# Attention and mixture of experts on one core: moving the first turns of each head pair behind its own joint tile, and the third and fourth tiles' turns into one run

## The chip, the cores and the metric

The kernel runs on one core of a Trainium2 chip. A core has TensorE (PE in the profile, its weight loads PEld), VectorE (DVE), ScalarE (ACT), GpSimd (POOL) and SyncE (SP), which here issues transfers. Each engine has its own queue and works through it in order; semaphores tie the queues together. The metric is the device time of one execution in microseconds (us), lower being better.

## The reference

Causal attention with a decay over 8 batches, 8 heads, 576 positions and 64 channels a head, then a mixture of eight experts, of which each token takes one:

```python
scores = scale * np.matmul(q, k.transpose(0, 1, 3, 2))
log_f = np.log(np.clip(f, 0.0001, 1.0))
cum = np.cumsum(log_f, axis=-1)
decay = cum[:, :, :, None] - cum[:, :, None, :]
scores = np.where(causal, -1000000000.0, scores + decay)
attn = softmax(scores)                    # over the last axis
attn_out = np.matmul(attn, v)
...
x = attn_out.transpose(0, 2, 1, 3).reshape(B * S, H * D)
logits = x @ w_gate
expert_idx = np.argmax(logits, axis=1)    # gate_w: its softmax probability
...
h = np.maximum(xe @ w1[e], 0.0)
out[mask] = gate_w[mask, None] * (h @ w2[e])
```

## The kernel before

Attention runs over 32 pairs of heads, four to a batch, in `attention_all`; the experts follow (`Moe`), from about 320 us on. The attention loop has a step for each pair n and each i from 0 to 6 (two more rounds of it drain the pipeline). The order that the code issues in is pinned on every engine (`InOrder`), so each engine's queue is what the loop writes.

A pair's scores come as tiles of 128 queries, named head and row block: 03 and 13 are 512 keys wide, 02 and 12 are 384 wide (with 00 and 10, 128 wide, in the same PSUM bank), 01 and 11 are 256 wide and share a bank. The last 64 queries of both heads make one joint tile (J), in two halves of 288. For each tile TensorE does the score matmuls (`smm`, L414, two passes of operands named qk and k,q), VectorE adds the mask and takes the row minimum while it copies the scores to SBUF (`s_red`, L421, a reduction and a short read of its accumulator), and ScalarE takes the exponential in place (`s_exp`, L428). `s_steps(n)` lists these for i = 0 to 5: 03; 13; 02 with 00; 12 with 10; 01 with 11; J.

The probabilities are then turned, that is transposed on TensorE against the identity (`turn`, L477), into a PSUM bank and copied from there to the tile aT (L471 on VectorE, L473 on ScalarE). `t_steps(n - 1)` lists the turns of the pair before, one item for each i of pair n: first 03, second 13, third 02 with 00, fourth 12 with 10, then `t_one` for 01 with 11, then the joint tile. ScalarE copies the 512- and 384-wide ones, VectorE the two 128-wide ones (00, 10) and t_one's. The turns share the pool `ps_t` of two PSUM banks: a turn's bank is that of the turn two before it. Score tiles share three banks (`ps_s`).

At i = 1 of pair n, `av(n - 2)` multiplies the turned probabilities by v (L553), into the banks `ps_v` and `ps_m`, one each, and ScalarE copies them out (L561).

Once a batch's four pairs are through, `fin_tasks(b)` spreads its routing over the next four pairs and a little beyond, in a list of (pairs later, i, task), with g the number of the first of them:

- `fin_x(b, t)` turns a block of x rows (`xT`) and VectorE scales it into a row tile (L599), which goes to DRAM three steps later (`c.later`, L607). Its bank is `ps_v` or `ps_m`.
- `fin_gate` (L623) and `fin_logits` make the router's logits: turns of gT, then VectorE's products (L641).
- `softmax`, `expert`, `gate`, `rank`, `slot`, `hi`, `lo` and `table` rank the tokens for the experts. `rank` has matmuls L935 and L937 and VectorE's L942 to L950; `hi` a one-hot on VectorE (L972) and five products on GpSimd (L979); `lo` a one-hot on VectorE (L986); `table` the matmuls L993.

Also in a pair, GpSimd splits the next pairs' operands into high and low parts (L330, L369, L379), and VectorE does one cast of k (L373, `k_first`).

Of the kernel before, what the change touches and what calls it, by code (L numbers as in the profile page):

```python
# [174 lines left out]
def attention_all(c, tc, qkT, va, vb, f, wgd, x_dram, batch_done, more_consts, extra):  # L175
# [15 lines left out]
    with ExitStack() as st:  # L191
# [15 lines left out]
        def step(f):  # L207

            if pe_last:
                with tc.issue_after(pe_last[0]):  # L210
                    f()
            else:
                f()
# [370 lines left out]
        def fin_x(b, t, scalar=False, bank=None):  # L584
            xT, rinv = xTws[b], rinvs[b]
            qs, qn = QS[t], QN[t]

            px = psum(ps_s if (b, t) == (B - 2, 0) or b == B - 1 and t > 1
                      else bank or fin_bank[0])
            for p in range(NPAIR):  # L590
                turn(px[:qn, P * p : P * p + P], xT[:, p, qs : qs + qn])
            xr = row_tile(c)
            if scalar:
                for h in range(H):
                    hs = slice(h * HD, h * HD + HD)
                    nc.scalar.activation(xr[:qn, hs], px[:qn, hs], AF.Copy,
                                         scale=rinv[:qn, t, h : h + 1])
            else:
                V.tensor_tensor(  # L599
                    xr[:qn].rearrange("q (h d) -> q h d", d=HD),  # L600
                    px[:qn].rearrange("q (h d) -> q h d", d=HD),
                    rinv[:qn, t, :].unsqueeze(2).to_broadcast([qn, H, HD]), ALU.mult,
                )
            r0 = b * S + qs

            def write():
                nc.sync.dma_start(x_dram[r0 : r0 + qn, :], xr[:qn])  # L607


            if b < B - 2:  # L610
                c.later.append([3, write])
            else:
                write()
# [16 lines left out]
        def fin_logits(b, part, bank=None):  # L630
            rinv = rinvs[b]
            if part == 0:
                lgs[b] = (c.ps_r[:, 0:40].rearrange("p (t e) -> p t e", e=8),
                          sm.tile([P, 5, 8, 8], F32, name="gq", bufs=1))
            lg, gq = lgs[b]
            pg = psum(bank or fin_bank[0])
            tiles = (0, 1, 2, 3) if part == 0 else (4,)
            for i, t in enumerate(tiles):
                turn(pg[:, P * i : P * i + P], gTw[part][:, P * i : P * i + P])
            for i, t in enumerate(tiles):  # L640
                V.tensor_tensor(  # L641
                    gq[:, t],
                    pg[:, P * i : P * i + P].rearrange("q (h e) -> q e h", e=16)[:, 0:8, :],
                    rinv[:, t, :].unsqueeze(1).to_broadcast([P, 8, 8]), ALU.mult,
                )
            if part == 1:
                V.tensor_reduce(lg, gq, AX.X, ALU.add)
# [4 lines left out]
        def fin_tasks(b):  # L652

            (softmax, expert, gate, rank, slot, hi, lo, table), after = batch_done(
                b, lambda: lgs[b][0]
            )
            fx = [lambda t=t: fin_x(b, t, b == B - 1 and t > 0) for t in range(5)]
            lg = [lambda p=p: fin_logits(b, p) for p in range(2)]  # L660
            g = NPAIR * b + 6
            if b == B - 1:
                return dict(fx=fx, lg=lg, softmax=softmax, expert=expert, gate=gate,
                            rank=rank, slot=slot, hi=hi, lo=lo, table=table,
                            logits=lambda: fin_gate(b))
            r = [(0, 3, lg[0]), (1, 0, lambda: fin_logits(b, 1, ps_m)), (1, 1, softmax),
                 (1, 1, expert), (2, 1, gate)]

            if b < B - 2:
                among[g + 1, 3] = [rank]  # L670
                late = int(b < B - 1 - LATE)
                r += [(0, 2, fx[0]), (0, 4, fx[1]), (2, 2, fx[2]), (2, 3, fx[3]), (3, 1, slot),
                      (3 + late, 1, lo), (3, 2, hi), (4, late, table)]
                r += [(4, 0, lambda: fin_x(b, 4, bank=ps_m)) if late else (3, 3, fx[4])]
            else:
                r += [(2, 0, rank), (2, 1, slot), (2, 2, fx[0]), (2, 3, hi), (2, 3, lo),
                      (2, 3, fx[1]), (2, 4, fx[2]), (2, 5, fx[3]), (2, 6, fx[4]),
                      (3, 0, table)]
            for dn, i, f in r + after:

                at, i = (among, ~i) if i < 0 else (tasks, i)
                at.setdefault((g + dn, i), []).append(f)
# [40 lines left out]
        def c_writes():  # L723
# [4 lines left out]
            sp_dma(ck[:, :, 1, 0:512], cwf[NPR:NH, :, 0:512])  # L728
            sp_dma(ck[:, :, 1, 512:], cwf[NPR:NH, :, S:640])
        tasks, among, c.later, order = {}, {}, [], InOrder(tc)  # L730
        c.note = note
        for n in range(NP + 2):
            b, p = divmod(n, NPAIR)
            if n < NP and p == 0:
                xTs[b], xTws[b] = (
                    t["xT", (b + 1) % 2].rearrange("p (n s) -> p n s", s=S)
                    for t in (c.values, c.words)
                )
                ssums[b] = sm.tile([P, 5, H], F32, name="ssum")
                V.memset(ssums[b][64:128, 4, :], 1.0)  # L740
                jsums[b] = sm.tile([P, NPAIR], F32, name="jsum")
            ss = s_steps(n) if n < NP else []
            ts_ = t_steps(n - 1) if 0 < n <= NP else []
            for i in range(7):
                for x in c.later:
                    x[0] -= 1
                while c.later and c.later[0][0] <= 0:
                    c.later.pop(0)[1]()
                if n == 0:
                    if i == 0:  # L750
                        first_q(1)
                        late_consts()
                    elif i == 2:
                        second_q(1)
                    elif i == 3:
                        first_k(1)
                    elif i == 5:
                        second_k(1)
                elif n + 1 < NP:
                    if i == 0 and n > 1:  # L760
                        load_c(n + 1)
                    elif i == 0:
                        c_rows(2, 0)
                        c_rows(2, 1)
                        load_pair(3)
                        c_writes()
                    elif i == 2:
                        copies(n + 1)
                if i in (2, 4) and 2 <= n < 5:
                    next(c.more, None)  # L770
                if i == 5 and n + 2 < NP:
                    q_parts(n + 2)
                if i == 5 and n == 2:
                    load_gate()
                if i == 3 and n < NP:
                    load_v(n)
                if i == 2 and 0 < n < NP - 3:
                    load_pair(n + 3)
                s_, e_ = ss[i] if ss else (None, None)
                if s_:  # L780
                    step(s_)
                for f in among.pop((n, i), []):
                    step(f)
                if ts_ and ts_[i]:
                    step(ts_[i])

                if e_:
                    e_()
                if i == 1 and 0 < n and n + 1 < NP:
                    k_first(n + 1)  # L790
                if i == 1 and 2 <= n:
                    step(lambda: av(n - 2))
                    av_out()


                    fb, fp = divmod(n - 2, NPAIR)
                    if fp == 0 and 1 <= fb:
                        step(lambda: fin_gate(fb - 1))
                        fin_tasks(fb - 1)
                    elif fp == NPAIR - 1 and fb == B - 1:  # L800
                        todo = fin_tasks(fb)

                fin_bank[0] = (ps_v, ps_m)[i % 2]
                for f in tasks.pop((n, i), []):
                    step(f)
                at = {(0, 1): 0, (1, 0): 1, (1, 1 if b == B else 5): 2}.get((p, i))
                if n >= NPAIR and at is not None:
                    fin_sums(b - 1, at)
                if (n, i) == (NP, 0):
                    scores.close()  # L810
                for f in extra(n, i):
                    step(f)
                order.pin()
                if (n, i) == (NP + 1, 1):
                    break
# [961 lines left out]
```

## Time and profile before

| what | value |
|---|---|
| median of three runs | 791.38 us (791.35 to 792.48) |
| the profiled execution, its own time | 791.58 us |
| its span in the profile | 789.8 us |
| granted TensorE clock | 0.999 |
| PE, DVE, ACT, POOL busy | 768.5, 587.0, 511.2, 543.8 us |
| turns (L477), PE, first two head-0 tiles: 03 and 02 | 15.6 and 16.3 us in 128 turns each |

A row of the timeline has start and duration in us, engine, line, operation, what it writes and reads, shapes, count, and in brackets the idle time before it with what ended it. The 128x512 and the like after the operation are partitions and elements. Matmuls are pipelined and their ends are modelled, so TensorE is read by its starts. A group of waits has the waiting engine and line, what it waited for, the sum in us, the count, and the longest.

### The profile page before, as it was taken

Reading aid. Unit: us, or ns where it says so; the run is one execution under the profiler, and the core shown is the slowest. Engines: PE = TensorE matmul, PEld = TensorE weight load, DVE = VectorE, ACT = ScalarE, POOL = GpSimd, SP = SyncE. Lnnn points to the kernel's source line nnn. Section 1 sums busy time; section 2 is a strip of 40 time slices with the busy share of each in tenths; the row PEclk is TensorE's granted clock in tenths of the full one; section 3 lists DMA queues with packets and bytes.
Section 4 is the critical chain, followed back from the end, with each engine's and each line's share of the span. In section 5 each row is a group of like instructions: output and inputs, shape, how many; then the busy total and the mean of one; then the engine's idle time right before and its main releaser. Section 6 shows DMA issues by size and latency. Waiting matters only on the chain.

```text
span 789.8 us, 16191 instructions
## 1 busy us (share of the span) xinstructions
PE 768.5 (97%) x5496; PEld 672.3 (85%) x5496; DVE 587.0 (74%) x1654; ACT 511.2 (65%) x1278; POOL 543.8 (69%) x466
## 2 busy tenths in 40 slices
PE   4999999999999999999999999999999999999996
PEld 3888888888888888888999899898898998998985
DVE  6688989898989899755589848578497487485630
ACT  6798888888888888944466546366366465463621
POOL 6999898989898989753487647556565575475311
PEclk9999999999999999999999999999999999999999
DMA  7998877787787874533445362353433433523200
GB/s 182 224 208 188 198 182 189 188 185 183 180 200 174 203 173 120 178 114 118 124 134 160 107 198 83 103 189 93 143 105 107 156 93 107 181 70 110 98 28 32
DMA packets 66825, 114.70 MB, mean 145 GB/s; under 512 B 8295, under 2 KB 39015, under 8 KB 63412
## 3 DMA queue, kind: packets, MB, share of 16 engines
q1 hardware_dynamic: 59700, 93.71, 45.8%
q0 software_dynamic: 6400, 19.93, 7.8%
q8 instruction: 44, 0.72, 0.4%
q14 instruction: 41, 0.34, 0.1%
q10 hardware_dynamic: 640, 0.01, 0.0%
HBM read 94.05 MB, written 20.55 MB: 145 GB/s over the span
## 4 chain that ended last, share of the span: by engine, by line
PE 89%; DVE 6%; ACT 2%; POOL 1%; SPq 1%; issue 1%; DMA 1%; POOLq 0%; DVEq 0%; ACTq 0%
PE ps L1200 29%; PE ps L1400 19%; PE ps L414 14%; PE ps L553 10%; PE ps L477 9%; PE ps L1170 4%; PE pr L1400 1%; DVE sc L421 1%; PE ps L1356 1%; DVE qk L373 1%; ACT sc L428 1%; DVE aT L471 1%; SPq L217 1%; ACT aT L473 1%; PE pr L993 1%
## 5 line engine op out<-in xcount | busy, mean ns | idle before, releaser
L428 ACT ACTIVATE sc<-sc,nmx 128x512 f32<-128x512 f32 (+3 forms) x256 | 142.3, 558 | 7.3 <-DVE nmx L421 5.5
L414 PE MATMUL ps<-qk 128*128 128x288 f32 (+4 forms) x384 | 124.9, 356 | 10.7 <-ACT qk L355 10.4
L421 DVE CUSTOM_DVE_ANT_0 sc<-ps,mask 128x512 f32<-128x512 f32 (+3 forms) x256 | 115.1, 483 | 16.4 <-PE ps L414 15.1
L1200 PE MATMUL ps<-w_0w,hhw 128*128 128x512 f32 x280 | 112.9, 403 | 0.0
L1400 PE MATMUL ps<-X_0w,w1s 128*128 128x320 f32 x504 | 111.7, 309 | 0.0
L1200 PE MATMUL ps<-w_0w,hl 128*128 128x512 f32 x280 | 110.8, 396 | 0.0
L1200 PE MATMUL ps<-w_1w,hhw 128*128 128x512 f32 x280 | 110.4, 394 | 0.0
L414 PE MATMUL ps<-k,q 68*128 68x288 f32 (+4 forms) x384 | 107.2, 327 | 1.5 <-DMA q<-xT0w 1.5
L1208 POOL DMA_INDIRECT out<-y,si_fast x37 | 37.3, 1009 | 96.6 <-ACT y L1207 87.6
L473 ACT COPY aT<-ps 128x512 f32<-128x512 f32 (+1 forms) x156 | 82.8, 531 | 20.4 <-PE ps L477 20.2
L553 PE MATMUL ps<-aT,va_t 128*64 128x256 f32 (+3 forms) x896 | 94.6, 354 | 0.0
L330 POOL TENSOR_TENSOR k<-raw,qk 64x1152 fp32r<-64x1152 f32 x30 | 79.8, 2659 | 18.4 <-DVE qk L373 18.4
L330 POOL TENSOR_TENSOR qk<-raw,qk 64x1280 fp32r<-64x1280 f32 x30 | 88.1, 2936 | 2.4
L1400 PEld LDWEIGHTS ps<-X_0w,w1s 128*128 128x128 f32 x504 | 84.3, 188 | 0.0
L414 PEld LDWEIGHTS ps<-qk 128*128 128x128 f32 x384 | 71.1, 197 | 14.1 <-ACT qk L355 10.4
L1207 ACT ACTIVATE y<-ps,g_fast 128x512 f32<-128x512 f32 x37 | 25.5, 690 | 87.0 <-PE ps L1200 64.9
L553 PEld LDWEIGHTS ps<-aT,va_t 128*64 128x64 f32 x896 | 58.9, 137 | 26.0 <-issue 0.7
L1400 PE MATMUL ps<-X_1w,w1s 128*128 128x320 f32 x252 | 77.9, 309 | 0.0
L414 PEld LDWEIGHTS ps<-k,q 68*128 68x128 f32 x384 | 72.7, 199 | 3.0 <-issue 2.6
L1447 POOL TENSOR_TENSOR u<-u,u 128x320 f32<-128x320 f32 x27 | 23.7, 878 | 60.6 <-DVE u L1445 60.3
L1200 PEld LDWEIGHTS ps<-w_0w,hl 128*128 128x128 f32 x280 | 52.5, 187 | 12.8
L1200 PEld LDWEIGHTS ps<-w_1w,hhw 128*128 128x128 f32 x280 | 52.8, 189 | 11.0
(242 smaller groups left out, 1900.6 us busy)
## 6 DMA issues: line engine op xcount, KB each, us to landing
raw<-in_qkT SPq DMA_DIRECT2D x52, 608.0 KB
w1r<-in_w SPq DMA_DIRECT2D x112, 128.0 KB
w<-in_w SPq DMA_DIRECT2D x28, 512.0 KB
va_t<-in_va SPq DMA_DIRECT2D x32, 256.0 KB
x_dram<-row SPq DMA_DIRECT2D x32, 256.0 KB
raw<-in_qkT SPq DMA_DIRECT2D x12, 320.0 KB
wraw<-in_w SPq DMA_DIRECT2D x7, 512.0 KB
raw<-in_qkT SPq DMA_DIRECT2D x12, 288.0 KB
```

Of the source, the lines that this page charges most:

```text
L330: return eng.tensor_tensor(o, raws[n][p0 : p0 + 64, c0:c1], ops[n][0][p0 : p0 + 64, c0:c1].bitcast(F32), ALU.subtract,)
L414: note(nc.tensor.matmul(out, ql[:, q0 : q0 + P], kl[:, j, k0 : k0 + kw], start=(i == 0), stop=(i == last),))
L421: V.tensor_tensor_reduce(dst[:, 0 : src.shape[1]], src, m, -0.125, init, ALU.add, ALU.min, nms[n][:, col : col + 1],)
L428: nc.scalar.activation(x, x, AF.Exp, bias=nms[n][:, col : col + 1], scale=-1.0, accum_out=acc)
L473: nc.scalar.copy(dst, src)
L477: note(nc.tensor.transpose(out.bitcast(F32R), words, c.identr))
L553: c.last_av = note(nc.tensor.matmul(pv[j * HD : (j + 1) * HD, q0 - qa : qb - qa], l, r, start=(blk == 0), stop=(blk == nb - 1),))
L1170: c.note(nc.tensor.matmul(ph[:, 0:n], w[:, wi, fs], x[xi][:, kt, :], start=(k == 0), stop=(k == 3 * KT - 1),))
L1200: c.note(nc.tensor.matmul(py, rows(hi_, ft), w[wi], start=(ft + k == 0), stop=(ft == FT - 1 and k == 2),))
L1207: nc.scalar.activation(y, py, AF.Copy, scale=g[:, s : s + 1])
L1208: nc.gpsimd.indirect_dma_start(out=self.out, out_offset=bass.IndirectOffsetOnAxis(ap=si[:, s : s + 1], axis=0), in_=y, in_offset=None, bou ...
L1400: self.nc.tensor.matmul(bank[:, 0:HN], w[:, wi, mat, kt], x[xi][:, kt, :], start=start and k == 0, stop=k == 5, skip_group_check=True,)
```

## The change

The first turns of a pair (03) move from the next pair's i = 0 to the pair's own i = 5, right behind the joint tile's turns of its predecessor. The third turns (02, 00) move from i = 2 to i = 3, so that they and the fourth run together. The exponentials of the third tile (02, 00) are held until after the fourth turns' copies. Of the routing, the logits' second part moves from the start of the next pair to i = 5, the first and third rows of x move a step later, behind the fourth turns, the fifth row moves from the next pair's i = 0 to i = 5, and each row has its bank fixed. The last batches keep their banks.

```diff
+            fx = [(lambda t=t, k=k: fin_x(b, t, bank=k))
+                  for t, k in enumerate((ps_v, ps_v, ps_v, ps_m, ps_m))] if b < B - 2 else fx
-            r = [(0, 3, lg[0]), (1, 0, lambda: fin_logits(b, 1, ps_m)), (1, 1, softmax),
+            r = [(0, 3, lg[0]), (0, 5, lambda: fin_logits(b, 1, ps_m)), (1, 1, softmax),
                  (1, 1, expert), (2, 1, gate)]
...
-                r += [(0, 2, fx[0]), (0, 4, fx[1]), (2, 2, fx[2]), (2, 3, fx[3]), (3, 1, slot),
+                r += [(0, 3, fx[0]), (0, 4, fx[1]), (2, 3, fx[2]), (2, 3, fx[3]), (3, 1, slot),
                       (3 + late, 1, lo), (3, 2, hi), (4, late, table)]
-                r += [(4, 0, lambda: fin_x(b, 4, bank=ps_m)) if late else (3, 3, fx[4])]
+                r += [(3, 5 if late else 3, fx[4])]
...
+        turns = {1: (1,), 3: (2, 3), 4: (4,), 5: (5,)}
+        held = []
...
+            if ts_:
+                ts_[0] = None
...
-                if ts_ and ts_[i]:
-                    step(ts_[i])
-
-                if e_:
+                for k in (turns if n < NP else {i: (i,)}).get(i, ()) if ts_ else ():
+                    if ts_[k]:
+                        step(ts_[k])
+                if i == 5 and n < NP:
+                    step(t_steps(n)[0])
+
+                if e_ and i == 2 and ts_:
+                    held.append(e_)
+                elif e_:
+                    while held:
+                        held.pop()()
                     e_()
```

On TensorE, in a pair without rows of x at this place, from the third score tile (02 with 00) to t_one's scores; sc_02w and sc_12w are the third and fourth turns:

```order
 L414 MATMUL ps<-qk_1300 128x128
 L414 MATMUL ps<-k_1_208,q_1_206 128x128
-L477 MATMUL ps<-identr,sc_02w 128x128 x4
 L414 MATMUL ps<-qk_1300 128x384
 L414 MATMUL ps<-k_1_208,q_1_206 128x384
 L414 MATMUL ps<-qk_1300 128x128
 L414 MATMUL ps<-k_1_208,q_1_206 128x128
+L477 MATMUL ps<-identr,sc_02w 128x128 x4
 L477 MATMUL ps<-identr,sc_12w 128x128 x4
 L414 MATMUL ps<-qk_1300 128x256
```

The third turns now stand behind the fourth tile's scores, in one run with the fourth turns.

On VectorE at the same place of such a pair; the ISA rows are the reductions of a tile and their reads, the copies of 128x128 are those of 00 and 10:

```order
 L421 ISA sc_02_73,nmx<-ps,mask 128x128
 L421 ISA nmx 128x1
-L471 COPY aT_91<-ps 128x128
 L421 ISA sc_12_79,nmx<-ps,mask 128x384
 L421 ISA nmx 128x1
 L421 ISA sc_12_79,nmx<-ps,mask 128x128
 L421 ISA nmx 128x1
-L471 COPY aT_91<-ps 128x128
+L471 COPY aT_91<-ps 128x128 x2
 L421 ISA sc_01_75,nmx<-ps,mask 128x256
 L421 ISA nmx 128x1
```

The copy of 00 now stands behind the fourth tile's two reductions.

On TensorE, from the joint turns of the pair before (sc_Jw) into the next pair's first scores:

```order
 L477 MATMUL ps<-identr,sc_Jw 68x128
 L477 MATMUL ps<-identr,sc_Jw 128x128 x4
+L477 MATMUL ps<-identr,sc_03w 128x128 x4
 L414 MATMUL ps<-qk_325 128x512
 L414 MATMUL ps<-k_0_207,q_0_205 128x512
-L477 MATMUL ps<-identr,sc_03w 128x128 x4
 L414 MATMUL ps<-qk_325 128x512
 L414 MATMUL ps<-k_0_207,q_0_205 128x512
```

The first turns (sc_03w) moved from between the two 512-wide score tiles to right behind the joint turns, ahead of both.

## The prediction

> **What bounds the kernel now.** I read the engines' shares on the page first, then the chain that ended last, then TensorE's own waits, and last, for four attention pairs in a row, the stretch from a pair's third score tile to the next pair's attention times values.
>
> ```profile
> PE 768.5 (97%) x5496; PEld 672.3 (85%) x5496; DVE 587.0 (74%) x1654; ACT 511.2 (65%) x1278; POOL 543.8 (69%) x466
> PE 89%; DVE 6%; ACT 2%; POOL 1%; SPq 1%; issue 1%; DMA 1%; POOLq 0%; DVEq 0%; ACTq 0%
> ...
> PE pr L993 <- DVE Ar L986: 2.1, 5, 0.4
> ...
> PEld ps L477 <- DVE aT L471: 3.2, 16, 0.2
> ```
>
> TensorE is busy 97% of the span and holds 89% of the chain. Inside attention its only listed waits are the five at the routing table (L993), 0.42 us each. The last row is the warning: 16 times a turn's weight load already sat still until VectorE had copied an older turn out of PSUM (L471).
>
> The four stretches, with columns of width, then busy time of PE, PEld, DVE, ACT and POOL, then the granted clock (1.00 throughout):
>
> ```profile
> 182.85:189.10 6.25, 6.25 (x58) 5.88 (x54) 5.26 (x24) 5.50 (x19) 5.84 (x7) 1.00 0.71 157
> 194.02:201.31 7.29, 7.29 (x65) 6.82 (x62) 6.60 (x28) 4.84 (x16) 7.15 (x4) 1.00 0.37 124
> 204.18:210.57 6.39, 6.39 (x59) 5.90 (x55) 5.80 (x32) 5.50 (x21) 6.31 (x3) 1.00 0.89 182
> 213.44:220.15 6.71, 6.71 (x61) 6.31 (x57) 6.36 (x28) 5.51 (x20) 6.48 (x6) 1.00 0.87 208
> ```
>
> I call them by what rides along: the plain pair, the logits pair (two rows of x and the logits), the rank pair, the rows pair (two rows of x). They repeat with each batch. TensorE never stops in them, and VectorE rests only 0.99, 0.69, 0.59 and 0.35 us. So TensorE sets the pace, and VectorE, which empties PSUM, is close behind: an order that makes TensorE need a bank earlier, or VectorE free it later, costs at once.
>
> **The change part by part.** First the saving. TensorE's rows of the plain pair:
>
> ```profile
> 182.85 0.44 PE L414 MATMUL ps<-qk 128*128 128x384 f32 x1
> ...
> 183.82 0.41 PE L414 MATMUL ps<-qk 128*128 128x384 f32 x1
> 184.07 0.34 PE L414 MATMUL ps<-k,q 68*128 68x384 f32 x1
> 184.25 0.22 PE L414 MATMUL ps<-qk 128*128 128x128 f32 x1
> ...
> 185.31 0.29 PE L477 MATMUL ps<-identr,sc_01w 128*128 128x128 f32 x2
> ...
> 186.74 0.54 PE L477 MATMUL ps<-identr,sc_Jw 128*68 128x128 f32 x5
> 187.12 0.46 PE L414 MATMUL ps<-qk 128*128 128x512 f32 x1
> ...
> 188.19 0.45 PE L414 MATMUL ps<-qk 128*128 128x512 f32 x1
> 188.48 0.39 PE L414 MATMUL ps<-k,q 68*128 68x512 f32 x1
> 188.71 0.46 PE L477 MATMUL ps<-identr,sc_13w 128*128 128x128 f32 x4
> ```
>
> Starts are compared, since ends are modelled. A score matmul right behind a turn takes 0.25 us (183.82 to 184.07), its equal behind another score matmul 0.18 (184.07 to 184.25); at 512 columns 0.29 against 0.23. The new order takes two such switches out of each pair: the fourth tile's scores now follow the third's, and the second 512-wide tile follows the first. That is 0.07 + 0.06 = 0.13 us a pair. For 31 pairs that alone is 4.0 us.
>
> [...]
>
> Now the price. The turns share two PSUM banks in rotation, so a turn needs the bank of the turn two before it, and its copies out. VectorE's rows of the plain pair:
>
> ```profile
> 183.69 0.56 DVE L421 CUSTOM_DVE_ANT_0 sc<-ps,mask 128x384 f32<-128x384 f32 x1 [0.65 <-PE ps L414]
> 184.17 0.08 DVE L421 DVE_READ_ACCUMULATOR2_ANT nmx<- 128x1 f32 x1
> ...
> 184.38 0.08 DVE L421 DVE_READ_ACCUMULATOR2_ANT nmx<- 128x1 f32 x1
> 184.53 0.29 DVE L471 COPY aT<-ps 128x128 f32<-128x128 f32 x1
> 184.74 0.36 DVE L972 TENSOR_TENSOR eqh<-pr,iotah 128x200 bf16<-128x200 f32 x1
> 185.01 0.55 DVE L421 CUSTOM_DVE_ANT_0 sc<-ps,mask 128x384 f32<-128x384 f32 x1
> ...
> 186.10 0.41 DVE L421 CUSTOM_DVE_ANT_0 sc<-ps,mask 128x256 f32<-128x256 f32 x1
> ...
> 186.78 0.69 DVE L471 COPY aT<-ps 128x512 f32<-128x512 f32 x1
> ```
>
> A tile's two reductions take 0.48 + 0.21 = 0.69, a small copy 0.21 to the next start (0.29 to its end), the one-hot (L972) 0.27, the two 256-wide reductions 0.68, the 512-wide copy 0.69. VectorE starts 0.84 after the third tile's first matmul, because it waits for the scores, and will again.
>
> *Plain pair.* The small copy of the third turns, which frees the bank of t_one's turns (sc_01w), now stands behind the one-hot and the fourth tile's reductions: it ends at 0.84 + 0.69 + 0.27 + 0.69 + 0.29 = 2.78. TensorE wants the bank at 185.31 - 182.85 - 0.07 = 2.39. Wait 0.39; behind it queue t_one, the joint scores and all that follows on TensorE. Net 0.39 - 0.13 = +0.26. Before, the copy ended at 184.82, half a microsecond ahead of need.
>
> The logits pair needs rows of its own, three of VectorE's and three of TensorE's:
>
> ```profile
> 194.83 0.56 DVE L421 CUSTOM_DVE_ANT_0 sc<-ps,mask 128x384 f32<-128x384 f32 x1
> ...
> 197.44 0.61 DVE L641 TENSOR_TENSOR gq<-ps,rinv 128x64 f32<-128x64 f32 x4
> 197.96 0.41 DVE L421 CUSTOM_DVE_ANT_0 sc<-ps,mask 128x256 f32<-128x256 f32 x1
> ...
> 197.46 0.50 PE L477 MATMUL ps<-identr,xT0w 128*128 128x128 f32 x4
> ...
> 200.14 0.25 PE L477 MATMUL ps<-identr,gT1w 128*128 128x128 f32 x1
> 200.36 0.50 PE L414 MATMUL ps<-qk 128*128 128x512 f32 x1
> ```
>
> and so do the rank pair (206.83 to 208.73) and the rows pair (from 216.81), TensorE's and VectorE's:
>
> ```profile
> 206.83 0.29 PE L477 MATMUL ps<-identr,sc_01w 128*128 128x128 f32 x2
> ...
> 208.26 0.54 PE L477 MATMUL ps<-identr,sc_Jw 128*68 128x128 f32 x5
> 208.73 0.47 PE L414 MATMUL ps<-qk 128*128 128x512 f32 x1
> ...
> 206.90 0.20 DVE L942 TENSOR_TENSOR rk<-pr,rk 128x48 f32<-128x48 f32 x1
> ...
> 207.62 0.29 DVE L471 COPY aT<-ps 128x128 f32<-128x128 f32 x1
> ...
> 216.81 0.68 DVE L599 TENSOR_TENSOR row<-ps,rinv 128x512 f32<-128x512 f32 x1
> 217.41 0.41 DVE L421 CUSTOM_DVE_ANT_0 sc<-ps,mask 128x256 f32<-128x256 f32 x1
> ...
> 218.39 0.47 PE L414 MATMUL ps<-qk 128*128 128x512 f32 x1
> ```
>
> *Logits pair.* Both rows of x go through the one bank ps_v, one turn apart now instead of two. The first row leaves it when VectorE has done, from 0.81: four reductions 1.38, two copies 0.42, the logits' products 0.52 (197.44 to 197.96), the row itself 0.68, together 3.81. TensorE wants it at 197.46 - 194.02 - 0.07 = 3.37. Wait 0.44. A wait of before goes: one gate turn took 0.22 (200.14 to 200.36) where turns are 0.08 apart (five in 0.38), so 0.14. Net 0.44 - 0.13 - 0.14 = +0.17.
>
> *Rank pair.* The rank's operations (0.72, 206.90 to 207.62) now stand ahead of both small copies: 0.84 + 1.38 + 0.72 + 0.29 = 3.23, against 206.83 - 204.18 - 0.07 = 2.58. Wait 0.65. The joint turns took 0.47 there against 0.38 in the plain pair; that 0.09 goes. Net +0.43. If the routing work ahead holds VectorE longer than 0.84, the wait grows.
>
> *Rows pair.* Two rows (0.60 each, 216.81 to 217.41) run ahead of the 256-wide reductions and t_one's copy, and the moved first turns want that copy's bank right behind the joint turns: 0.84 + 1.38 + 0.42 + 1.20 + 0.68 + 0.69 = 5.21, against 218.39 - 213.44 - 0.07 = 4.88. Wait 0.33, net +0.20. In the other pairs TensorE has by then been held up enough for that copy.
>
> *Table.* The plain pair's one-hot loses the small copy ahead of it, so GpSimd, fed by it, and the cast and one-hot behind GpSimd come no later, while TensorE comes 0.26 later: the wait of 0.42 at L993 shrinks by 0.26 to 0.42. I take all of it, -0.42.
>
> Together 0.26 + 0.17 + 0.43 + 0.20 - 0.42 = +0.64 us for four pairs. Six batches take this course: 3.8, plus 0.42, as only five of them have the table's wait: +4.3. The pairs without routing (first five, last two) win 0.13 and lose 0.84 + 1.38 + 0.29 - 2.39 = 0.12: nothing.
>
> What I cost at nothing: the third turns' exponentials, held back on ScalarE behind the fourth turns' copy, are read a pair later; without that cover they would push the joint copy, whose bank the next fourth-score turns need. The stores of the moved rows shift by a turn at most on SP's queue, with pair loads behind them that are used a pair later. The logits' second part and the fifth row move from behind a 512-wide tile to before it, on the same engines.
>
> The profiled execution took 791.58 us around a span of 789.8; 791.58 + 4.3 = 795.9. The median of the three runs is 0.2 lower, so 795.7.
>
> **The rivals.** *Faster.* The banks come free before TensorE needs them: VectorE runs its block faster than I add up from single rows. The 16 waits of the first view speak against it: a bank was already met late with a 512-wide score tile more between. Were no wait left, 31 x 0.13 and the five table waits would be gained: 4.0 + 2.1 = 6.1, so 785.3. It decides where the new waits, 1.81 us for four pairs by my sum, are under 0.90, half of it.
>
> *No change.* The savings for four pairs are 4 x 0.13 + 0.14 + 0.09 + 0.42 = 1.17; were the waits as much, between 0.90 and 1.44, the time stays at 791.4.
>
> [...]
>
> *ScalarE late.* In the plain and rank pairs it rests only 0.75 and 0.89 us a stretch. If the held exponentials make its joint copy late, the turn behind the second 512-wide tile waits too; at 0.15 us a pair that is 31 x 0.15 = 4.7 more, 800.4.
>
> **How the numbers follow.** A measurement of this kernel can tell about 0.2%, 1.6 us. My forecast has 0.53, faster 0.14, no change 0.18, the weights 0.07, ScalarE 0.08. So slower by over 0.2% has 0.68. The forecast's own range, with each of four waits uncertain by 0.1 us in six batches (2.4), is 793.3 to 798.1. Taking in no change and the slower ones, and the near part of faster, gives 788.5 to 800.5.
>
> **What would show it.** Right: TensorE idle on L471 ahead of sc_01w in plain and rank pairs (0.4 and 0.65), on the row operation ahead of xT turns in the logits pair (0.44), on L471 ahead of sc_03w in the rows pair (0.33); no wait at the table; the four stretches 6.5, 7.5, 6.8 and 6.9 us long instead of 6.25, 7.29, 6.39 and 6.71. Wrong: those turns directly behind the scores with no gap, and each stretch 0.13 us shorter than before.

## The result, and the profile after

| | before | after |
|---|---|---|
| median | 791.68 us (791.35 to 792.48, 6 runs) | 803.23 us (801.48 to 804.74, 6 runs) |
| the profiled execution, its span | 791.58, 789.8 us | 802.01, 800.2 us |

The ratio is 1.0144, with a 95% interval from 1.0129 to 1.016: slower by 1.44%. The forecast was 795.7, with a range from 788.5 to 800.5. Of the 11.5 us between the medians, 10.4 stand between the two profiled executions, which both had the full clock (0.999). The rest goes with the clock: the two runs of after at 0.999 took 801.48 and 802.01 us, the three at 0.996 and 0.997 took 803.64 to 804.74.

The page of the changed kernel, its busy times and its chain:

```profile
PE 769.8 (96%) x5496; PEld 672.0 (84%) x5496; DVE 592.2 (74%) x1654; ACT 508.6 (64%) x1278; POOL 543.7 (68%) x466
PE 82%; DVE 8%; DMA 4%; ACT 3%; issue 1%; POOL 1%; SPq 0%; ACTq 0%; POOLq 0%; DVEq 0%
```

TensorE's busy time is nearly what it was (768.5 us before). Its share of the chain fell from 89% to 82%: waits came between. TensorE's waits, then those of its weight loads (what is waited for, the sum in us, times, longest):

```profile
PE ps L477 <- DVE aT L471: 6.4, 17, 0.5
PE ps L477 <- DVE row L599: 3.6, 6, 0.6
...
PE ps L477 <- ACT aT L473: 0.6, 1, 0.6
```

```profile
PEld ps L477 <- DVE aT L471: 11.4, 25, 0.7
...
PEld ps L477 <- ACT aT L473: 2.6, 4, 1.0
```

The five waits at the table are gone, and 23 waits of turns on VectorE stand in their place. The four stretches, same columns as before:

```profile
187.93:194.60 6.67, 6.43 (x57) 5.91 (x53) 5.70 (x24) 5.36 (x18) 6.07 (x8) 1.00 0.56 116
199.03:206.89 7.86, 7.26 (x65) 6.80 (x62) 7.17 (x30) 5.68 (x19) 7.57 (x4) 1.00 0.65 174
209.76:216.67 6.91, 6.42 (x59) 5.88 (x56) 6.12 (x32) 5.58 (x20) 6.77 (x4) 1.00 0.78 155
219.54:226.77 7.23, 6.84 (x62) 6.39 (x58) 6.34 (x26) 5.91 (x19) 6.34 (x7) 1.00 0.85 204
```

They are 0.42, 0.57, 0.52 and 0.52 us longer than before; 0.26, 0.17, 0.43 and 0.20 were forecast. From the plain pair's values to the logits pair's third tile, across the table, it is 4.43 us (194.60 to 199.03) instead of 4.92: 0.49 shorter, 0.42 forecast. The sum is +1.54 us for four pairs instead of +0.64. The places, on TensorE; the row ahead of each waiting one shows where it came from:

```profile
190.24 0.28 PE L414 MATMUL ps<-k,q 68*128 68x256 f32 x1
190.76 0.36 PE L477 MATMUL ps<-identr,sc_01w 128*128 128x128 f32 x2 [0.24 <-DVE aT L471]
190.96 0.33 PE L477 MATMUL ps<-identr,sc_11w 128*128 128x128 f32 x2
...
202.12 0.29 PE L477 MATMUL ps<-identr,sc_01w 128*128 128x128 f32 x2
202.24 0.33 PE L477 MATMUL ps<-identr,sc_11w 128*128 128x128 f32 x2
203.18 0.54 PE L477 MATMUL ps<-identr,xT0w 128*128 128x128 f32 x4 [0.60 <-DVE row L599]
...
212.26 0.29 PE L414 MATMUL ps<-k,q 68*128 68x256 f32 x1
213.03 0.36 PE L477 MATMUL ps<-identr,sc_01w 128*128 128x128 f32 x2 [0.49 <-DVE aT L471]
...
224.08 0.54 PE L477 MATMUL ps<-identr,sc_Jw 128*68 128x128 f32 x5
225.01 0.53 PE L477 MATMUL ps<-identr,sc_03w 128*128 128x128 f32 x4 [0.39 <-DVE aT L471]
```

All four stand where the forecast put them. By starts, less the distance that the same two instructions have without a wait (0.12, 0.17, 0.12, 0.38), they are 0.40, 0.77, 0.65 and 0.55 us, 2.37 together; forecast were 0.39, 0.44, 0.65 and 0.33, together 1.81.

### The profile page after: what moved, and what is told of

It is laid out like the page before. It is cut to its first block, busy times and chain, and to the rows that moved or that the text cites. A ratio compares the mean times of both kernels' runs of the same rounds, so it can differ in the third digit from the quotient of the medians.

```text
span 800.2 us, 16161 instructions
## 1 busy us (share of the span) xinstructions
PE 769.8 (96%) x5496; PEld 672.0 (84%) x5496; DVE 592.2 (74%) x1654; ACT 508.6 (64%) x1278; POOL 543.7 (68%) x466
## 4 chain that ended last, share of the span: by engine, by line
PE 82%; DVE 8%; DMA 4%; ACT 3%; issue 1%; POOL 1%; SPq 0%; ACTq 0%; POOLq 0%; DVEq 0%
PE ps L1215 28%; PE ps L1415 19%; PE ps L553 10%; PE ps L414 10%; PE ps L477 6%; PE ps L1185 4%; DVE sc L421 3%; DMA va_t<-in_va 3%; ACT aT L473 2%; PE pr L1415 1%; DVE row L599 1%; PE ps L1371 1%; DVE aT L471 1%; PE ps L623 1%; ACT sc L428 1%
## 5 line engine op out<-in xcount | busy, mean ns | idle before, releaser
L414 PE MATMUL ps<-qk 128*128 128x288 f32 (+4 forms) x384 | 120.1, 348 | 10.6 <-ACT qk L355 10.4
L421 DVE CUSTOM_DVE_ANT_0 sc<-ps,mask 128x512 f32<-128x512 f32 (+3 forms) x256 | 112.6, 484 | 22.7 <-PE ps L414 21.1
L473 ACT COPY aT<-ps 128x512 f32<-128x512 f32 (+1 forms) x156 | 78.4, 540 | 43.0 <-PE ps L477 43.0
L553 PE MATMUL ps<-aT,va_t 128*64 128x256 f32 (+3 forms) x896 | 94.0, 353 | 0.0
L414 PEld LDWEIGHTS ps<-qk 128*128 128x128 f32 x384 | 71.4, 198 | 14.4 <-ACT qk L355 10.4
L553 PEld LDWEIGHTS ps<-aT,va_t 128*64 128x64 f32 x896 | 58.7, 137 | 25.6 <-issue 0.2
```

What stands on the lines that cost most here:

```text
L414: note(nc.tensor.matmul(out, ql[:, q0 : q0 + P], kl[:, j, k0 : k0 + kw], start=(i == 0), stop=(i == last),))
L421: V.tensor_tensor_reduce(dst[:, 0 : src.shape[1]], src, m, -0.125, init, ALU.add, ALU.min, nms[n][:, col : col + 1],)
L473: nc.scalar.copy(dst, src)
L553: c.last_av = note(nc.tensor.matmul(pv[j * HD : (j + 1) * HD, q0 - qa : qb - qa], l, r, start=(blk == 0), stop=(blk == nb - 1),))
```

## The experiments

Each row below is one batch of four pairs in the profiled execution: the distance in us between the first attention-times-values matmuls (L553) of neighbouring pairs, named by the pair whose stretch it ends with. The logits pair's entry contains the table. The batch is the same in all kernels, and the clock was full there.

| kernel | logits | rank | rows | plain | four pairs |
|---|---|---|---|---|---|
| before | 12.20 | 9.27 | 9.61 | 9.11 | 40.18 |
| after | 12.28 | 9.79 | 10.11 | 9.54 | 41.72 |
| e1 first turns alone | 11.71 | 9.71 | 10.04 | 9.59 | 41.06 |
| e2 run alone | 11.63 | 10.00 | 9.78 | 9.57 | 40.99 |
| e3 routing alone | 13.18 | 9.18 | 10.06 | 9.14 | 41.56 |
| e9 after, nothing held | 12.95 | 9.82 | 10.76 | 9.97 | 43.51 |
| e4 after, row first | 11.78 | 10.07 | 10.09 | 9.54 | 41.47 |
| e5 after, rank later | 12.29 | 9.67 | 10.10 | 9.54 | 41.61 |
| e6 after, row later | 12.29 | 9.77 | 9.68 | 9.54 | 41.27 |
| e7 after, all three | 11.78 | 9.69 | 9.68 | 9.55 | 40.70 |
| e10 after, copies | 11.82 | 9.98 | 9.74 | 9.74 | 41.27 |
| e11 e7, copies | 11.49 | 9.79 | 9.75 | 9.74 | 40.76 |
| e13 e7, one copy | 11.98 | 9.85 | 9.84 | 9.57 | 41.23 |
| e8 before, one-hot | 11.87 | 9.27 | 9.60 | 9.11 | 39.83 |
| e12 before, copies | 11.74 | 9.21 | 9.58 | 9.17 | 39.70 |
| e14 before, both | 11.75 | 9.21 | 9.58 | 9.17 | 39.71 |
| e15 before, one copy | 11.82 | 9.12 | 9.63 | 9.23 | 39.80 |

**One part at a time.** e1: the first turns alone behind the joint turns.

```diff
+            if ts_:
+                ts_[0] = None
...
+                if i == 5 and n < NP:
+                    step(t_steps(n)[0])
```

> The kernel before, with the first turns alone moved behind the pair's own joint turns. If the cost is waits on turn banks that VectorE frees late: the first turns need t_one's copy out, which in the rows of before ends 0.41 (plain), 0.09 (logits), 0.61 (rank) and 0.45 us (rows pair) after TensorE would be there; less the saved switch and two old waits, about +1.3 us for four pairs and 0.6 a pair without routing, some +10 us, 802. If the cost came from ScalarE, by the held exponentials: no change, 791.7, as nothing is held here.

e2: the third turns alone to the fourth's, with the exponentials held.

```diff
+        turns = {0: (0,), 1: (1,), 3: (2, 3), 4: (4,), 5: (5,)}
...
+                for k in (turns if n < NP else {i: (i,)}).get(i, ()) if ts_ else ():
```

> The kernel before, with the third turns alone moved to the fourth's, and the third tile's exponentials held as in the change. Bank waits: t_one's turns wait for the small copy, 0.40 in the plain and 0.65 in the rank pair, none in the other two, where a row of x turns in between; the table's wait goes; about +0.5 us for four pairs and 0.1 to 0.3 for a pair without routing, 795.5. ScalarE late: all of the loss shows here, 803.

e3: the places and banks of the routing alone (the changed lines of `r` and `fx`, nothing of the turns).

> The kernel before, with the routing tasks alone (rows of x, their banks, the logits' second part) where the change puts them. Bank waits: the second row of x waits for ps_v some 0.5 us in the logits pair, less 0.14 of an old wait, six times: +2.5 us, 794. ScalarE late: no change, 791.7.

Measured against 791.78 before: e1 799.52, ratio 1.0092 (1.0075 to 1.0109); e2 798.83, 1.0082 (1.0066 to 1.0099); e3 799.74, 1.0103 (1.0086 to 1.0119). The bank waits that were expected came, but the sizes were missed: about 10, 4 and 2.5 us of loss were expected, and 7.7, 7.1 and 8.0 were measured. TensorE's waits in e1, e2 and e3:

```profile
PE ps L477 <- DVE aT L471: 9.3, 26, 0.7
```

```profile
PE ps L477 <- DVE aT L471: 5.5, 11, 0.7
```

```profile
PE ps L477 <- DVE row L599: 5.8, 6, 1.0
PE ps L414 <- DVE nmx L421: 2.1, 7, 0.6
PE pr L995 <- DVE Ar L988: 2.0, 5, 0.4
```

Each part alone brings a wait on VectorE, and nearly the same loss. In e1 it stands ahead of sc_03w in the plain, rank and rows pairs, in e2 ahead of sc_01w in the plain and rank pairs, in e3 ahead of a row's turns (xT0w) in the logits pair, and, not expected, 0.24 us ahead of a 512-wide score matmul in the rows pair, which waits for a reduction of VectorE (L421). Four pairs lose 0.88, 0.81 and 1.38 us, 3.07 together, but only 1.54 in the change as made: the parts don't add up. A likely reason, not shown, is that TensorE, once held, meets the later copies ready. The batches are the cleaner measure here, since the profiled executions of e1 and e2 also stood idle at the start, and with a lower clock behind it (last section). e3 shows also that the routing's new places, without a turn moved, leave the table's wait as it was (L995 is L993 of before): that one goes where TensorE comes later, or VectorE sooner.

**The held exponentials.** e9: as after, but `e_()` at once.

```diff
-                if e_ and i == 2 and ts_:
-                    held.append(e_)
-                elif e_:
+                if e_:
```

> The changed kernel without the hold: the third tile's exponentials stand before the third and fourth turns' copies on ScalarE. Bank waits: ScalarE then copies the third turns out about 0.6 us later, VectorE's small copies stand behind those, and t_one's turns wait longer still: slower than the change, 806 to 812. ScalarE late by the hold: the exponentials run earlier, the joint copy too, and most of the loss comes back, about 796.

Measured 820.15, ratio 1.0355 (1.0334 to 1.0376), beyond the 806 to 812 that were expected. VectorE's small copies then wait for ScalarE's, which stand behind the exponentials:

```profile
189.26 0.83 ACT L473 COPY aT<-ps 128x384 f32<-128x384 f32 x2
189.75 0.67 DVE L471 COPY aT<-ps 128x128 f32<-128x128 f32 x2 [0.62 <-ACT aT L473]
```

Holding them is what keeps the change from costing more than twice as much (3.33 us instead of 1.54 for four pairs), and it is not the cause of the loss in these pairs. The traces also show a link that the forecast had not counted: no small copy started while ScalarE copied from the same bank. In before and after alike, each of the last 60 small copies starts 31 ns or more behind the end of ScalarE's copy out of its bank, and 34 of them within 33 ns of it. In e9 VectorE sat idle 13.9 us ahead of its turn copies (L471) until a copy of ScalarE was through.

**One wait at a time.** All three start from the changed kernel. e4: the first row of x ahead of the logits' products.

```diff
+            r = [(0, 3, fx[0])] if b < B - 2 else []
...
-                r += [(0, 3, fx[0]), (0, 4, fx[1]), (2, 3, fx[2]),
+                r += [(0, 4, fx[1]), (2, 3, fx[2]),
```

> The changed kernel, with the logits pair's first row of x ahead of the logits' products on TensorE and VectorE. Bank waits: that row leaves ps_v 0.53 us earlier, so the wait of 0.60 ahead of the second row (0.77 by starts) falls to about 0.25, six times: 3.2 us less than the change, 800. If the row's bank did not set the time: as the change, 803.2.

e5: the rank behind the fourth turns, so behind the small copies on VectorE.

```diff
-                among[g + 1, 3] = [rank]
+                r.append((1, 3, rank))
```

> The changed kernel, with the rank behind the third and fourth turns instead of ahead of them, so that VectorE's small copies come before the rank's operations. Bank waits: t_one's turns find the bank 0.7 us earlier and wait about 0.05 instead of 0.65: six times 0.6, 3.6 us less than the change, 799.6. If not: 803.2.

e6: the fourth row of x a step later.

```diff
-(2, 3, fx[3])
+(2, 4, fx[3])
```

> The changed kernel, with the rows pair's second row of x one step later, behind t_one's turns, so that VectorE copies t_one's bank out 0.6 us earlier. Bank waits: the wait of 0.55 ahead of the first turns goes: six times, 3.3 us less than the change, 800. If not: 803.2.

Measured against 792.02: e4 802.56, ratio 1.0139 (1.0122 to 1.0157); e5 801.91, 1.013 (1.0111 to 1.0148); e6 800.95, 1.0109 (1.0093 to 1.0126). e6 does what it should: 0.43 us of the rows pair goes. e4 gains 0.50 in the logits pair and gives 0.28 back in the rank pair, and e5 gains only 0.12 of the rank pair's wait. Where it went, e4's rank pair and then e5's:

```profile
211.66 0.36 PE L477 MATMUL ps<-identr,sc_01w 128*128 128x128 f32 x2 [0.74 <-DVE aT L471]
```

```profile
215.30 0.54 PE L477 MATMUL ps<-identr,sc_03w 128*128 128x128 f32 x4 [0.34 <-DVE aT L471]
```

In e4 the wait of 0.49 ahead of sc_01w in the rank pair grew to 0.74: TensorE arrives sooner, VectorE does not. In e5 that wait is gone and 0.34 stands ahead of sc_03w instead. VectorE has the same work in the stretch, and in both runs what is taken from one of its copies is put on the next.

**All three waits.** e7 joins e4, e5 and e6.

> The changed kernel with three moves at once: the first row of x ahead of the logits' products, the rank behind the fourth turns, the fourth row of x one step later. Theory (each wait stands on VectorE at its own place, so the moves add up): by the single runs a batch of four pairs gets shorter by 0.21 + 0.10 + 0.42 = 0.73 us, for six batches 4.4, so the profiled execution comes from 802.0 to 797.6. Rival (VectorE has a backlog, so a wait taken away comes back further on): 799 to 801, with L471 ahead of sc_03w or sc_01w still idle in the rank and logits pairs.

Measured 796.65 against 792.15, ratio 1.0068 (1.0045 to 1.0091): about half of the loss is undone. Four pairs got 1.02 us shorter, not 0.73: the rank moved behind the copies takes back what e4 had lost in that pair. What stays in the four pairs is the plain pair's wait, 0.24 idle as in after, and 0.16 in the rank pair; pairs without routing take 9.41 us, as in after:

```profile
188.72 0.37 PE L477 MATMUL ps<-identr,sc_01w 128*128 128x128 f32 x2 [0.24 <-DVE aT L471]
...
212.28 0.53 PE L477 MATMUL ps<-identr,sc_03w 128*128 128x128 f32 x4 [0.16 <-DVE aT L471]
```

**VectorE relieved.** e10: as after, with the two small copies of a pair on ScalarE. e11: the same in e7. e12: the same in the kernel before.

```diff
-                lambda: t_tiles(n, [(0, 2), (0, 0)], e + "v"),
-                lambda: t_tiles(n, [(1, 2), (1, 0)], e + "v"),
+                lambda: t_tiles(n, [(0, 2), (0, 0)], e + e),
+                lambda: t_tiles(n, [(1, 2), (1, 0)], e + e),
```

> The changed kernel with the two 128-wide copies of a pair's third and fourth turns on ScalarE instead of VectorE. Theory (the new waits are VectorE's lateness: the small copies stand behind its reductions and wait for ScalarE's copies of the same bank): VectorE gets 0.42 to 0.60 us a pair back, the banks of the third turns come free at about 190.35 where TensorE wants them at 190.36, so the waits of 0.40, 0.77, 0.65 and 0.55 shrink to some 0.2 together, a batch goes from 41.7 to about 39.7, and the time is about 790. Rival (ScalarE becomes late with 0.5 us more a pair, its joint copy holds the next turns): 799 to 804, with waits on L473 in place of those on L471.

> The three moves and the small copies on ScalarE together. Theory (VectorE's lateness is all that the new order costs): no wait of TensorE on L471 or on the row operation is left in the four stretches, and the time is 786 to 789, below the kernel before. Rival (TensorE waits for ScalarE then): 796 to 800.

> The kernel before with its four small copies a pair's two on ScalarE. Theory (in the order of before TensorE waits only at the table): only the table's wait shrinks, as its one-hot starts 0.2 us sooner, five times, so 790.5. Rival 1 (the order of before pays hidden prices for late copies too): below 788. Rival 2 (ScalarE late): over 794.

Measured: e10 803.6, ratio 1.0155 (1.0137 to 1.0172); e11 799.54, 1.0095 (1.008 to 1.0111); e12 789.26, 0.996 (0.9947 to 0.9974). In e10 the waits on VectorE are down to one of 0.2, and the rival came true:

```profile
PE ps L477 <- ACT aT L473: 7.8, 16, 1.2
...
PE ps L477 <- DVE aT L471: 0.2, 1, 0.2
```

```profile
189.06 1.20 ACT L473 COPY aT<-ps 128x384 f32<-128x384 f32 x4 [1.20 <-PE ps L477]
...
193.72 0.53 PE L477 MATMUL ps<-identr,sc_13w 128*128 128x128 f32 x4 [0.35 <-ACT aT L473]
```

ScalarE stands idle for 1.20 us until the run of turns is through, then has four copies and all exponentials of the third to fifth tiles in one piece, and the joint copy behind them, which starts at 193.09, holds sc_13w. e11 has the same wait there, 0.35 in the plain and 0.31 in the rank pair. Their profiled executions are longer at the end too: from TensorE's last matmul to the end of the span, while the last tile is scaled and stored, e10 takes 8.1 us and e11 7.7, before 6.4 and after 6.5. In the order of before the same copies on ScalarE gain 0.48 us for four pairs, nearly all of it at the table, though a pair without routing takes 9.16 us there, in before 8.88 to 9.22. So in these four pairs ScalarE is not short of time; in the run it gets its work too late.

**One copy, and the better kernel.** e13: e7 with only the copy of 00 on ScalarE. e14: the kernel before with both copies there, and the table's one-hot ahead of VectorE's copies. e15: before with that one-hot ahead and the copy of 00 on ScalarE. e8, run earlier: before with the one-hot ahead and nothing else. The `~` puts a task of a step between that step's scores and its turns.

```diff
-(3, 2, hi)
+(3, ~2, hi)
```

> The three moves of e7 and, of the two small copies, only that of 00 (third turns) on ScalarE; that of 10 stays on VectorE. Theory (the grouped order has too little slack on both engines, and the wait goes to the one that is later): the wait of 0.40 on L471 ahead of sc_01w goes, ScalarE's joint copy comes 0.2 us sooner than with both copies on it, so of its 0.35 ahead of sc_13w some 0.15 stay; a batch of four pairs gets from 40.7 to about 40.0, the time 792 to 793. Rival A (no engine is late any more): 788 to 790. Rival B (each copy on ScalarE costs as much as it saves on VectorE): 796 to 800.

> The kernel before, with one VectorE row moved: the one-hot that feeds GpSimd's products goes ahead of the small copy of 00, in one pair of each batch; all else is word for word. If the gain of the change lies in the table's wait: GpSimd starts up to 0.36 us earlier, the cast behind it too, and the wait of 0.42 at the table falls to about 0.1, five times: 1.5 us less than before, 790.2. If that wait is set otherwise (the cast not released earlier): no change, 791.7.

> The kernel before with both small copies on ScalarE and the table's one-hot (L972) ahead of VectorE's copies. Theory (in the order of before TensorE waits for neither copying engine, only at the table): the two gains are the same wait at L993 for the most part, 0.49 and 0.35 us a batch of four pairs alone, at most 0.6 together, so 788.5 to 789.3. Rival (they add up in full): 787.5.

> The kernel before with the one-hot ahead and only the copy of 00 on ScalarE. Theory: the table's wait is gone with either; ScalarE's joint copy keeps 0.2 us more slack, so 788.5 to 789.5, within 0.5 of the kernel with both. Rival (VectorE still sets the stretch of the logits or rows pair): 790.

Measured: e13 801.93, ratio 1.0116 (1.0091 to 1.0141); e8 790.31, 0.998 (0.9969 to 0.9991); e14 789.86, 0.9969 (0.9959 to 0.9979); e15 793.29, 1.0018 (1.0006 to 1.003). My theory of e13 fell: four pairs got 0.53 us longer than in e7. VectorE's copy of 10 now waits for ScalarE's three copies, and what stands behind it is late: the logits, rank and rows pairs are 0.20, 0.16 and 0.16 us longer than in e7. That copy in the plain pair, and the wait in the rank pair:

```profile
191.93 0.29 DVE L471 COPY aT<-ps 128x128 f32<-128x128 f32 x1 [0.24 <-ACT aT L473]
...
215.88 0.53 PE L477 MATMUL ps<-identr,sc_03w 128*128 128x128 f32 x4 [0.60 <-DVE aT L471]
```

e8, e12 and e14 win the same wait: 0.35, 0.48 and 0.47 us for four pairs, not their sum. The weight loads' wait at the table was 2.9 us in before; in e8 it is 1.2, in e12 and e14 1.4.

e15 has as short a batch (39.80) but a longer time. In its profiled execution 2.6 us of that stand behind TensorE's last matmul: from there to the end of the span it takes 9.0 us, before 6.4. Why it is slower in all its runs stays open. e8, e12 and e14 beat both kernels; e12, with a letter changed in two lines, has the lowest median, though its interval overlaps with those of the other two.

## Why the prediction was wrong in size

Four pairs lost 1.54 us, where 0.64 was forecast. The mechanism and the four places were right; sizes of terms in the sum were not. Of the 7.5 us between 795.7 and 803.2, 5.1 lie in the six batches with routing, 1.0 outside them, which was put at nothing, and 1.4 in the runs (1.1 between the medians and the profiled executions, 0.3 in a higher median of before).

**The saving, 0.13 us a pair: the first step that failed.** It compared the wrong rows. 184.07 to 184.25 is the second pass (k,q) to its successor, 183.82 to 184.07 the first pass (qk) to the second; they differ also without a turn in between. Like for like, in after:

```profile
188.56 0.39 PE L414 MATMUL ps<-qk 128*128 128x384 f32 x1
188.79 0.34 PE L414 MATMUL ps<-k,q 68*128 68x384 f32 x1
...
192.65 0.50 PE L477 MATMUL ps<-identr,sc_03w 128*128 128x128 f32 x4
192.99 0.40 PE L477 MATMUL ps<-identr,xT1w 128*64 128x128 f32 x4
193.22 0.45 PE L414 MATMUL ps<-qk 128*128 128x512 f32 x1
193.51 0.39 PE L414 MATMUL ps<-k,q 68*128 68x512 f32 x1
193.74 0.39 PE L414 MATMUL ps<-qk 128*128 128x512 f32 x1
193.97 0.40 PE L414 MATMUL ps<-k,q 68*128 68x512 f32 x1
```

A 384-wide first pass takes 0.23 behind a score matmul (188.56 to 188.79) and 0.25 behind a turn: the switch costs 0.02, not 0.07. At 512 columns it is 0.29 (193.22) against 0.23 (193.74), the 0.06 that I took; but the four first turns behind other turns take 0.34 (192.65 to 192.99), and 0.30 behind a score matmul, as before had them:

```profile
187.65 0.46 PE L477 MATMUL ps<-identr,sc_03w 128*128 128x128 f32 x4
187.95 0.23 PE L477 MATMUL ps<-identr,xT1w 128*64 128x128 f32 x1
```

Over whole blocks of the plain pair: from the third tile to t_one's scores 1.90 before (182.85 to 184.75) and 1.88 after (187.93 to 189.81), from the joint turns to the values 2.36 (186.74 to 189.10) and 2.34 (192.26 to 194.60). The saving is 0.04 us in this pair, less than a third of the term. Read in the same way, and without the waits, these two blocks got 0.51 us shorter in the four pairs together, where 4 x 0.13 + 0.14 + 0.09 = 0.75 were taken. That is 0.24 of the missing 0.90. So 0.04 lies nearer to a grouping that saves nothing, the case called the weights in the forecast's chances, than to the 0.13 of my rows; why a switch costs so little was not shown.

**The waits: the larger step that failed.** Plain (0.40 for 0.39) and rank (0.65 for 0.65) were right. Logits and rows were short by 0.33 and 0.22, 0.55 together. VectorE's and ScalarE's rows of the logits pair:

```profile
200.81 0.86 ACT L473 COPY aT<-ps 128x384 f32<-128x384 f32 x2 [1.51 <-PE ps L477]
201.32 0.67 DVE L471 COPY aT<-ps 128x128 f32<-128x128 f32 x2
201.91 0.61 DVE L641 TENSOR_TENSOR gq<-ps,rinv 128x64 f32<-128x64 f32 x4
202.44 0.68 DVE L599 TENSOR_TENSOR row<-ps,rinv 128x512 f32<-128x512 f32 x1
```

The step that failed is "two copies 0.42": they took 0.59 (201.32 to 201.91), each held until ScalarE's copy out of its bank was through. They started 2.29 after the third tile's first matmul instead of 2.19, and the turn followed the row's end (203.12) by 0.06. 0.17 + 0.10 + 0.06 is the missing 0.33. VectorE's rows of the rows pair:

```profile
221.79 0.67 DVE L471 COPY aT<-ps 128x128 f32<-128x128 f32 x2
...
222.39 1.28 DVE L599 TENSOR_TENSOR row<-ps,rinv 128x512 f32<-128x512 f32 x2
```

Here too the two copies took 0.60 (221.79 to 222.39), not 0.42, and the turn again started 0.06 behind the copy that it waited for (224.95 to 225.01); that is about the missing 0.22. In the plain pair the copies took 0.40 (190.42 to 190.82): the one-hot ahead of them had put them behind ScalarE's. VectorE's idle of 0.62 us in e9 and of 0.24 in e13, both ended by ScalarE's copies, agree with this; what makes one copy wait for the other was not shown.

**The restart.** The turns behind a wait went slower: sc_01w to sc_11w 0.20 (190.76 to 190.96) where it is 0.12 without one (202.12 to 202.24). I had it at nothing; it costs 0.08 in the plain pair and as much in the rank pair (213.03 to 213.24). Waits taken 0.56 too small, restarts of 0.16 left out and savings taken 0.24 too large, less the 0.07 that the table gave more, make 0.89 of the missing 0.90.

**Table, gate turn, held exponentials, ScalarE.** The table's term was right (-0.49 for -0.42). From the joint turns to the values the logits pair gained 0.17 and the rank pair 0.18, where 0.14 + 0.06 and 0.09 + 0.06 were taken. The held exponentials cost nothing in these four pairs, and e9 shows what the hold covers. The rival with a late ScalarE was wrong for these pairs (TensorE's one listed wait on it, 0.6 us, stands at 331 us), right for e10 and, as the next rows show, for the pairs without routing. The faster rival's premise, banks free in time, was refuted by the four rows.

**The pairs without routing and the start.** "Nothing" was wrong by 1.0 of the 10.4 us: the six batches hold 9.4 (2.08 in the first, which has no table, 1.50 to 1.55 in the next four, 1.24 in the last). The rest lies in the first and the last pairs. From after, the second 512-wide tile and the turns behind it in a pair without routing:

```profile
49.98 0.39 PE L414 MATMUL ps<-k,q 68*128 68x512 f32 x1
50.46 0.53 PE L477 MATMUL ps<-identr,sc_13w 128*128 128x128 f32 x4
```

These starts are 0.48 apart, in before 0.23 (50.65 to 50.88). The weight load of this turn waited for ScalarE: in the first 81 us the weight loads of turns wait 1.6 us for ScalarE's copies and 1.0 for VectorE's. ScalarE's joint copy starts 1.34 behind the joint turns (48.49 to 49.83), where it was 0.99 (49.14 to 50.13), and t_one's turns, waiting for VectorE, start 0.17 later too. So this pair takes 9.41 us (41.51 to 50.92) where before takes 8.88 (42.39 to 51.27). That is the mechanism of the rival with a late ScalarE; the forecast had counted only VectorE's small copy in these pairs. e2, with the third turns' move alone, has such waits too: its weight loads of turns wait 4.6 us for ScalarE's copies, ten times, where before has 0.7 us in two; whether the hold or the burst makes the copy late was not separated. The start gives part of the loss back: the first attention times values came 1.0 us sooner in after (31.87, in before 32.88), behind loads whose time varies (TensorE's waits for q sum to 0.5 us in e14 and 1.6 in e12).

The sign came out right because the two largest waits alone (1.42 us) exceed all the gains (0.51 and the table's 0.49). What stays open is whether the grouped order can be had without a late engine at all: e7, e10, e11 and e13 pushed the wait from VectorE to ScalarE and back, and the best of them, 796.65, is still above before.

## What to carry to other kernels

Here a run of like instructions on a full engine saved little (0.04 us in the plain pair), and it sent its results to the copying engines in a burst: ScalarE stood idle ahead of its copies for 43.0 us until turns were through, in before for 20.2, and behind the burst TensorE's turns waited 6.4 us for VectorE's copies. Count for each bank what stands ahead of its copy on that engine, and the copy of another engine out of the same bank. Compare durations only between instructions of the same kind and operands; and when one wait is taken away, look for it at the next instruction that needs the same late engine.

## What the runs showed of the hardware

**The clock fell behind an idle of 1.73 to 2.88 us.** Near 40 us the kernel waits for its first loads and what GpSimd makes of them, for a time that varies from run to run. In e1 it was 2.88 us, and the ten microseconds from 40 on had a clock of 0.83 (0.72 from 40 to 44, 0.86 from 44 to 48, then full again); in after, without such an idle, 1.00. The waiting row of e1, then the windows of e1 and of after (the clock is the third value from the end):

```profile
41.54 0.60 PE L414 MATMUL ps<-k,q 68*128 68x512 f32 x1 [2.88 <-POOL qk L369]
```

```profile
40.00:50.00 10.00, 8.46 (x64) 6.66 (x65) 4.57 (x14) 4.53 (x14) 9.75 (x11) 0.83 0.94 208
```

```profile
40.00:50.00 10.00, 9.68 (x85) 8.23 (x84) 9.00 (x28) 8.47 (x28) 9.73 (x12) 1.00 0.96 202
```

Of the profiled executions those with an idle of 1.73 us or more there (e9, e6, e2, e13, e1: 1.73, 1.89, 2.18, 2.47, 2.88; e9's is a wait for VectorE's copy, at 36.7) had a low clock behind it, those with 1.38 or less had not. That fits the lower clocks of some runs of after (0.996 and 0.997), and is not shown for them. In e9 the clock was 0.56 from 36 to 40 us and 0.50 from 40 to 44. The length of one idle was not shown to decide alone: e9's turns wait about 1.0 us for a row of x six times (5.8 together), and its clock was 1.00 from 100 to 200 us, over two of its batches, but 0.98 from 200 to 300. What else decides stays open.
